# A feed-forward layer on attention outputs: the first product of one of eight batches as seven products of half blocks

## The chip, the cores and the metric

The kernel runs on one core of one Trainium2 chip. The metric is the device time of one execution in microseconds (us). The engines are named as in the profile: PE is TensorE's matmul stream and PEld its weight loads, DVE is VectorE, ACT is ScalarE, POOL is GpSimd, SP is SyncE, which here issues the DMAs.

## The reference

Attention with a local window and some global tokens is followed by a feed-forward layer with a softplus between its two products. Cut to what matters:

```python
# 8 batches, 8 heads, 512 local and 32 global tokens, head size 64
out_g = sm(scale * q_g @ k_all.T) @ v_all                 # global rows see all tokens
s_ll = where(abs(i - j) <= 32, scale * q_l @ k_l.T, -1e9) # local rows: window of 32 and the global keys
out_l = sm(concat([s_lg, s_ll])) @ concat([v_g, v_l])
x = concat([out_g, out_l]) as (4352 tokens, 512)
h = x @ w_in                                              # w_in 512 x 2048
g = maximum(h, 0.0) + log1p(exp(-abs(h)))
out = g @ w_out                                           # w_out 2048 x 512
```

## The kernel before

**Numbers.** Every float32 operand of the feed-forward layer is split into a high and a low part, and each product of two operands is done as three matmuls: high by high, high by the weight's low part, low by the weight's high part. The two weight matrices come as 64-bit numbers, are converted on the chip in the first fifth of the run and then stay in SBUF as 16 tiles `wi0` to `wi15` and 16 tiles `wo0` to `wo15` (128 partitions, high and low part of 512 columns each).

**Stages.** Batches 0 to 7 have 512 local tokens each; "batch 8" is the 256 global tokens of all batches. For a batch and each of 16 blocks f of 128 hidden columns, the first product `h` is 4 row blocks j of `w_in` by 3 parts, 12 matmuls with 512 moving columns (`hpart`), 192 in a batch; in batch 8 the moving side is 256 wide. `act` then makes the softplus and its two parts: ACT takes abs, exp and ln (L557 to L559), DVE adds relu(h) straight from PSUM (L560, `scalar_tensor_tensor`, which frees the bank of `h`), ACT rounds to `gh` (L563) and POOL subtracts to `gl` (L565). The second product (`second`, `opart`) adds up four PSUM tiles `o0` to `o3` over f; a half step of it is 6 matmuls of 512 columns. `store` copies the four tiles out on DVE and ACT (L585, L583) and sends them.

**Attention beside it.** The attention of head pair m (four in a batch, from m = 9 on in batches 1 to 6, ahead of the batch that uses it) is woven in as pieces: `both_scores` (PE `s_ps`, then on DVE the mask addition L329 and L327 and the block maxima L335), `maxima` and `probs` (POOL folds L360, DVE transposes, POOL subtracts L386, ACT exp, DVE sums L392), `totals` (POOL folds, DVE reciprocal, three copies L401 and the transpose `rb` L403) and `values` with `normalise` (PE `v_ps`, DVE L423 to L428). What makes the order is a list of slots: a batch has 48 units of time, head pair m has its pieces at `12*m` plus 5, 14 and 17.5, and `ORDER` weaves one batch's `H` (a block of `h`), `O` (a block of the second product) and `G` (scores of a pair). A scheduler then fixes each engine's row of instructions; `order` rows below show that row. An engine takes its row strictly in order.

**PSUM.** Two banks with the tag `h` hold the `h` tiles and also the second half of each `s_ps` (`s_ps*_1_0` and `s_ps*_1_1`); one pair of banks with the tag `a` holds the first half of `s_ps` (`s_ps*_0`) and `v_ps`; four banks hold `o0` to `o3`. So a block of `h` that follows a `G` waits until DVE has added the mask to `s_ps*_1_0` (the first L327), and `s_ps*_0` waits until `normalise` has read a preceding `v_ps`.

**Batch 7** has no attention left beside it: blocks of `h` alternate with blocks of the second product that lag one or two blocks behind.

## Time and profile before

| what | value |
| --- | --- |
| median of 3 runs | 974.57 us (974.49 to 975.27) |
| the profiled execution | 975.65 us, of which the span of the profile is 973.9 us |
| granted TensorE clock, mean | 0.991 of full speed |
| PE busy | 944.3 us, 97% of the span |
| PEld (weight loads) busy | 762.1 us, 78% |
| DVE busy | 620.9 us, 64% |
| ACT busy | 507.4 us, 52% |
| POOL busy | 448.9 us, 46% |
| batch 7, first `h` to the first `h` of batch 8 | 834.08 to 922.97 us of the span, 384 matmuls |

The profile lists what each engine was busy with, the chain of waits that ended last, groups of equal instructions (with the mean time of one, and the idle time before them), and on request a timeline. In a timeline row the first number is the start in us, the second the time until the last of `xN` instructions ended; matmuls overlap each other, so the pace of a run of them is read from start to start. A DVE row "idle before <- releaser" names what the engine waited for.

### The profile page before, as it was taken

To read this page: it belongs to the slowest core of one execution; us is meant where nothing else is said; L and a number is where in the kernel's file an instruction comes from. 1 tells how busy PE (TensorE), PEld (TensorE's weight loads), DVE (VectorE), ACT (ScalarE), POOL (GpSimd) and SP (SyncE) were. 2 spreads that over 40 slices of the span, in tenths; PEclk is the share of its full clock that TensorE was granted. 3 is DMA by queue.
4 is the path that set the end of the run, shared out by engine and by line. 5 is a ranking of instruction groups with operands and counts; after the bars stand their busy time and mean duration, and the time that the engine had idled before them with its cause. 6 is when DMAs were issued, how large, how long until landed. Compare 5 with 4: busy or idle time off the path is not lost.

```text
span 973.9 us, 14402 instructions
## 1 busy us (share of the span) xinstructions
PE 944.3 (97%) x5235; PEld 762.1 (78%) x5239; DVE 620.9 (64%) x1271; ACT 507.4 (52%) x914; POOL 448.9 (46%) x634
## 2 busy tenths in 40 slices
PE   6798899999999999999999999999999999999998
PEld 3676677778878888888888888888888888888896
DVE  6887948766667776677667667776677666211211
ACT  5787766644464444454454445444445446444453
POOL 5866967634444444344344444444435344122221
PEclk9899999999999999999999999999999999999999
DMA  9824321121102111121112101211112100100000
GB/s 355 327 77 164 108 77 51 60 79 47 50 18 93 50 50 50 50 94 50 46 38 93 50 21 47 93 50 50 50 50 91 35 18 18 50 1 1 20 25 23
DMA packets 34327, 66.21 MB, mean 68 GB/s; under 512 B 7632, under 2 KB 11472, under 8 KB 34256
## 3 DMA queue, kind: packets, MB, share of 16 engines
...
q14 instruction: 30, 0.25, 0.1%
...
## 4 chain that ended last, share of the span: by engine, by line
PE 86%; DVE 6%; ACT 4%; POOL 3%; issue 1%; DMA 0%; POOLq 0%; ACTq 0%; DVEq 0%
PE o L127 38%; PE h L127 36%; PE s_ps L127 6%; PE v_ps L127 5%; ACT e L174 1%; POOL s L386 1%; DVE sums L171 1%; DVE wbitswi L505 1%; DVE woraw L508 1%; DVE wbitswo L505 0%; PE s0g L127 0%; DVE wiraw L508 0%; POOL wi L515 0%; PE s L127 0%; DVE wbitswo L503 0%
## 5 line engine op out<-in xcount | busy, mean ns | idle before, releaser
L127 PE MATMUL h<-xh,wi 128*128 128x512 f32 (+1 forms) x1152 | 345.1, 383 | 3.5 <-DVE e L560 2.3
L127 PE MATMUL o<-wo,gh 128*128 128x512 f32 x1088 | 346.1, 399 | 0.4 <-POOL wo L515 0.4
L565 POOL TENSOR_TENSOR gl<-e,gh 128x512 fp32r<-128x512 f32 (+1 forms) x152 | 180.6, 1192 | 269.5 <-ACT gh L563 239.4
L127 PEld LDWEIGHTS h<-xh,wi 128*128 128x128 f32 x1152 | 213.1, 189 | 49.4 <-DVE e L560 3.2
L127 PEld LDWEIGHTS o<-wo,gh 128*128 128x128 f32 x1088 | 200.3, 188 | 48.7 <-POOL wo L515 0.8
L127 PE MATMUL o<-wo,gl 128*128 128x512 f32 x544 | 215.3, 396 | 4.3 <-POOL gl L565 4.3
L127 PE MATMUL h<-xl,wi 128*128 128x512 f32 (+1 forms) x576 | 219.4, 381 | 0.0
L560 DVE SCALAR_TENSOR_TENSOR e<-h,e 128x512 f32<-128x512 f32 x136 | 92.7, 681 | 185.1 <-ACT e L559 166.9
L557 ACT ACTIVATE e<-h 128x512 f32<-128x512 f32 x136 | 80.9, 595 | 214.5 <-PE h L127 214.4
L386 POOL TENSOR_TENSOR s<-s,mb 128x320 f32<-128x320 f32 (+6 forms) x136 | 138.9, 1057 | 72.7 <-DVE mb L382 72.7
L563 ACT CAST gh<-e 128x512 fp32r<-128x512 f32 x136 | 84.0, 617 | 117.6 <-DVE e L560 117.6
L127 PEld LDWEIGHTS h<-xl,wi 128*128 128x128 f32 x576 | 108.7, 189 | 22.5
L127 PEld LDWEIGHTS o<-wo,gl 128*128 128x128 f32 x544 | 102.4, 188 | 29.2 <-POOL gl L565 5.5
L559 ACT ACTIVATE e<-e,one 128x512 f32<-128x512 f32 x136 | 98.4, 724 | 3.9
L392 DVE TRANSPOSE_TENSOR_REDUCE zt<-s 128x32 f32<-128x1024 f32 x52 | 64.6, 1243 | 49.3 <-ACT s L388 49.3
L558 ACT ACTIVATE e<-e 128x512 f32<-128x512 f32 x136 | 85.9, 632 | 2.9
L388 ACT ACTIVATE s<-s 128x1024 f32<-128x1024 f32 x52 | 55.1, 1059 | 30.9 <-POOL mt L318 26.3
L335 DVE TRANSPOSE_TENSOR_REDUCE mt<-s 128x32 f32<-128x1024 f32 x52 | 64.7, 1244 | 5.5 <-ACT s L322 3.9
L127 PEld LDWEIGHTS s_ps<-raw 64*128 64x128 f32 x728 | 54.6, 187 | 11.4 <-issue 8.9
L360 POOL COPY mt<-mt 32x75 f32<-32x75 f32 x78 | 18.9, 242 | 92.3 <-DVE mt L335 90.1
L127 PE MATMUL s_ps<-raw 64*128 64x192 f32 (+3 forms) x728 | 60.2, 308 | 0.5
L382 DVE STREAM_TRANSPOSE mb<-mt 128x512 f32<-128x512 f32 (+1 forms) x104 | 52.6, 562 | 3.1 <-ACT mt L373 2.5
...
## 6 DMA issues: line engine op xcount, KB each, us to landing
...
```

Of the source, the lines that this page charges most:

```text
L127: order["pe"] = after(nc.tensor.matmul(*a, **k), "pe").ins
L335: order["scores"] = nc.vector.tensor_reduce(windows(st["mt", m], 4 + 16 * g, 36, 2, 16), s.rearrange("p h (b k) -> p h b k", k=32), axis=A ...
L382: nc.vector.transpose(mb[:, :, o:o + 32 * n].rearrange("p h (s k) -> p h s k", k=32), windows(e, k, 21, 2, n).unsqueeze(3).to_broadcast([P ...
L386: nc.gpsimd.tensor_tensor(s[:, h, o:o + w], s[:, h, o:o + w], mb[:, h, q:q + w], op=ALU.subtract)
L388: nc.scalar.activation(s, s, AF.Exp, scale=0.125)
L392: nc.vector.tensor_reduce(windows(st["zt", m], 4 + 16 * g, 36, 2, 16), s.rearrange("p h (b k) -> p h b k", k=32), axis=AX.X, op=ALU.add, a ...
L557: nc.scalar.activation(e, ph, AF.Abs)
L558: nc.scalar.activation(e, e, AF.Exp, scale=-1.0)
L559: nc.scalar.activation(e, e, AF.Ln, bias=one)
L560: nc.vector.scalar_tensor_tensor(e, ph, 0.0, e, op0=ALU.max, op1=ALU.add)
L563: nc.scalar.copy(gh, e)
L565: nc.gpsimd.tensor_tensor(gl[:, c], e[:, c], gh[:, c].bitcast(F32), op=ALU.subtract)
```

## The change

Batch 7's first product no longer runs as 192 matmuls of 512 columns. `x` (512 tokens by 512) and each fourth part of `w_in` are cut into halves both ways, and the eight products of half blocks are replaced by seven products of sums (the Winograd form of Strassen's method). A product of half blocks is 2 row blocks by 3 parts, 6 matmuls of 256 columns; for 8 pairs p of column blocks (p and p + 8) that makes 8 x 7 x 6 = 336 matmuls of 256 columns. `three`, `six` and `seventh` hold the products, each followed by copies and sums: ACT copies four quarter regions from PSUM to an SBUF tile `c` (in the slot `wi3`), DVE adds twice (the new L682 and L691), and `act` then reads `c` in place of PSUM.

The sums of `w_in` are made ahead. There are 16 steps `mix` at slots 118, 132, 146 and so on, which falls in batches 1 to 5: two POOL operations of 128x512, one DVE addition, one ACT rounding, one DVE subtraction, and one DMA of 512 KB to a DRAM scratch tensor. They share one tile (tag `cv`, one buffer), so a step that starts a new tile waits for the DMA of the step before. Sixteen `mix_out` DMAs write the unchanged blocks there as well. Batch 7 (28 blocks) and batch 8 (16 blocks) read their weights back by 44 DMAs of 512 KB through a ring of 12 tiles in the slots `wi4` to `wi15`; a block is loaded when the block 12 places before it has been used. The sums of `x` (`sums_x`, 14 POOL operations) and their rounding (`operand_x`, 11 ACT and 11 DVE operations) take the place of `split_x` for batch 7. The slots of the last two head pairs (30 and 31) move from +14 and +17.5 to +12 and +14.5, and the output tiles of batches 6 and 7 move to another tag.

The core of the diff:

```diff
...
+FAST = 7
+RING = 12
+MIX0, MIX1 = 118, 14
+ORDER7 = (1, 2, 5, 4, 6, 3, 7)
...
-            g0, g1, mx, tot, val = SLOTS.get(m, (None, None, 12 * m + 5, 12 * m + TOT, 12 * m + VAL))
+            t = (12 * m + 5, 12 * m + TOT, 12 * m + VAL) if m < M - 2 else (12 * m + 5, 12 * m + 12, 12 * m + 14.5)
+            g0, g1, mx, tot, val = SLOTS.get(m, (None, None) + t)
...
+        for i in range(16):
+            ps.append((MIX0 + MIX1 * i, lambda i=i: (mix_out(i), mix(*MIXES[i]))))
         ps.sort(key=lambda t: t[0])
         return ps
+    MIXES = [(q, u) for q in (2, 3, 0, 1) for u in ("S3", "S1", "S2", "S4")]
+    mixed = {}
+    def mix_out(k):
+        q, kk = k // 2 % 4, k // 8 * 2 + k % 2
+        tc.keep_in_program_order(nc.sync.dma_start(out=mix_dram[8 * q + (0, 1, 7, 3)[kk]], in_=wi[k].rearrange("p u c -> p (u c)").bitcast(F32)))
+    def mix(q, what):
+        a11, a12, a21, a22 = wi[2 * q], wi[2 * q + 1], wi[2 * q + 8], wi[2 * q + 9]
+        if what in ("S3", "S1"):
+            mixed["o"] = pl.tile([P, 2, 512], F32R, tag="cv", name=f"mix{q}{what}", bufs=1)
+        o = mixed["o"]
+        x, y, op = {"S3": (a11, a21, ALU.subtract), "S1": (a21, a22, ALU.add),
+                    "S2": (o, a11, ALU.subtract), "S4": (a12, o, ALU.subtract)}[what]
+        lo = o[:, 1].bitcast(F32)
+        tc.keep_in_program_order(nc.gpsimd.tensor_tensor(o[:, 0].bitcast(F32), x[:, 0].bitcast(F32), y[:, 0].bitcast(F32), op=op))
+        tc.keep_in_program_order(nc.gpsimd.tensor_tensor(lo, x[:, 1].bitcast(F32), y[:, 1].bitcast(F32), op=op))
+        nc.vector.tensor_tensor(lo, lo, o[:, 0].bitcast(F32), op=ALU.add)
+        nc.scalar.copy(o[:, 0], lo)
+        nc.vector.tensor_tensor(o[:, 1], lo, o[:, 0].bitcast(F32), op=ALU.subtract)
+        nc.sync.dma_start(out=mix_dram[8 * q + {"S1": 2, "S2": 4, "S4": 5, "S3": 6}[what]], in_=o.rearrange("p u c -> p (u c)").bitcast(F32))
+    plan = [8 * q + i for b in range(FAST, B) for q in range(4) for i in range(7)]
+    plan += [8 * (k // 2 % 4) + (0, 1, 7, 3)[k // 8 * 2 + k % 2] for k in range(NF)]
+    ring = {}
+    def load_ring(i):
+        if i < len(plan):
+            t = ring[i] = pl.tile([P, 2, 512], F32R, tag=f"wi{4 + i % RING}", name=f"ring{i}", bufs=1)
+            nc.sync.dma_start(out=t.rearrange("p u c -> p (u c)").bitcast(F32), in_=mix_dram[plan[i]])
...
+    sums, xs = {}, {}
+    def sums_x(b, k):
+        if k == 0:
+            t = pl.tile([P, 4, 2, 256], F32, tag="s", name=f"sums{b}", bufs=2)
+            sums[b] = {5: t[:, 0], 6: t[:, 1], 7: t[:, 2], 4: t[:, 3]}
+        t1, t2, t3, t4 = (sums[b][i] for i in (5, 6, 7, 4))
...
+        for f, o, n, w in SECOND:
+            a = windows(lower, 160 if o == 0 else 384, w, n, w)
+            nc.gpsimd.tensor_tensor(cut(t1, o, n, w), f(lower), a, op=ALU.subtract)
+            nc.gpsimd.tensor_tensor(cut(t2, o, n, w), f(upper), cut(t1, o, n, w), op=ALU.subtract)
+            nc.gpsimd.tensor_tensor(cut(t3, o, n, w), f(upper), f(lower), op=ALU.subtract)
+        nc.gpsimd.tensor_tensor(cut(t4, 0, 2, 128), half_1(upper), cut(t2, 0, 2, 128), op=ALU.subtract)
+    def operand_x(b, i):
+        s = ORDER7[i]
+        if i < 4:
+            x = [pl.tile([P, 2, 256], F32R, tag=f"x{u}{i}", name=f"x{u}{b}_{s}", bufs=1) for u in "hl"]
+        else:
+            t = pl.tile([P, 2, 2, 256], F32R, tag=f"wi{i - 4}", name=f"x{b}_{s}", bufs=1)
+            x = [t[:, 0], t[:, 1]]
+        xs[s] = x
+        if s in sums[b]:
+            t = sums[b][s]
+            nc.scalar.copy(x[0], t)
+            nc.vector.tensor_tensor(x[1], t, x[0].bitcast(F32), op=ALU.subtract)
+            return
...
-                        mm(ph[:, o:o + T], lhsT=wi[ff // 2 * 2 + j // 2][:, u, fs], rhs=xv[j][:, :T],
+                        k = ff // 2 * 2 + j // 2
+                        w = wi[k] if b < B else ring[len(plan) - NF + k]
+                        mm(ph[:, o:o + T], lhsT=w[:, u, fs], rhs=xv[j][:, :T],
                            start=(j == 0 and i == 0 and o == 0), stop=(j == 3 and i == 2), skip_group_check=True)
+            if b == B and js[0]:
+                release(len(plan) - NF + 2 * f)
+                release(len(plan) - NF + 2 * f + 1)
+        def release(k):
+            if k >= 0:
+                load_ring(k + RING)
+        def product(b, p, i, ps, start, stop):
+            k = 28 * (b - FAST) + 7 * (p // 2) + i
+            w, x = ring[k], xs[ORDER7[i]]
+            for j in range(2):
+                fs = slice(256 * j + p % 2 * P, 256 * j + p % 2 * P + P)
+                for n, (u, v) in enumerate(((0, 0), (1, 0), (0, 1))):
+                    mm(ps, lhsT=w[:, u, fs], rhs=x[v][:, j], start=start and j == 0 and n == 0, stop=stop and j == 1 and n == 2,
+                       skip_group_check=True)
+            if p % 2:
+                release(k)
+            if p == 7 and b < B - 1:
+                operand_x(b + 1, i)
+        def three(b, p):
+            t = [ps_h.tile([P, 512], F32, tag="h", name=f"h{b}_{p}_{u}") for u in range(2)]
+            X, N, Q, V = t[0][:, 0:256], t[0][:, 256:512], t[1][:, 0:256], t[1][:, 256:512]
+            if "c" not in g:
+                g["c"] = pl.tile([P, 2, 512], F32, tag="wi3", name="c", bufs=1)
+            c = g["c"]
+            product(b, p, 0, X, True, True)
+            nc.scalar.copy(c[:, 0, 0:256], X)
+            product(b, p, 1, Q, True, True)
+            product(b, p, 2, V, False, True)
+            nc.scalar.copy(c[:, 1, 256:512], V)
+            g["h"] = t, X, N, Q, V
+        def six(b, p):
+            (t, X, N, Q, V), c = g["h"], g["c"]
+            product(b, p, 3, N, False, True)
+            product(b, p, 4, X, False, True)
+            nc.scalar.copy(c[:, 1, 0:256], N)
+            nc.scalar.copy(c[:, 0, 256:512], X)
+            product(b, p, 5, V, False, True)
+            nc.vector.tensor_tensor(c[:, 0], t[1], c[:, 0], op=ALU.add)
+            g["ps", b, p] = c[:, 0]
+            g["X"] = X
+            act(b, p)
+        def seventh(b, p):
+            X, c = g["X"], g["c"]
+            product(b, p, 6, X, False, True)
+            d = c[:, 1].rearrange("p (n w) -> p n w", n=2)
+            nc.vector.tensor_tensor(d, X.unsqueeze(1).to_broadcast([P, 2, 256]), d, op=ALU.add)
+            g["ps", b, p + 8] = c[:, 1]
         def act(b, f):
             ph = g.pop(("ps", b, f))
...
-            if f == 0 and b > 0:
+            if f == 0 and b > 0 and not FAST <= b < B:
                 items.append((b, 0, 0, lambda b=b: [split_x(b, j) for j in range(4)]))
+            if FAST <= b < B:
+                if f < 8:
...
+                    items.append((b, 3, 0, lambda b=b, f=f: three(b, f)))
+                    if mid:
+                        second(done, b)
+                        done += 1
+                    items.append((b, 3, 0, lambda b=b, f=f: six(b, f)))
...
+                    for step in "OHOAOO":
+                        if step == "O":
+                            k0 = next(k, None)
+                            if k0 is not None:
+                                second(k0, b)
+                                done += 1
+                        elif step == "H":
+                            items.append((b, 1, 0, lambda b=b, f=f: seventh(b, f)))
+                        else:
+                            items.append((b, 0, 0, lambda b=b, f=f: act(b, f + 8)))
+                continue
...
+                            if b == FAST - 1 and f % 2 and f > 4:
+                                items.append((b, 0, 0, lambda f=f: (load_ring(f - 5), load_ring(f - 4))))
+                            if b == FAST - 1 and f == NF - 1:
+                                items.append((b, 0, 0, lambda b=b: [sums_x(b + 1, k) for k in range(2)]))
+                                items.append((b, 0, 0, lambda b=b: [operand_x(b + 1, i) for i in range(7)]))
                         elif what == "O":
                             second(done, b)
                             second(done + 1, b)
...
```

**End of batch 6, PE.** `o6_*` is the second product of batch 6 (here with `wo8`), `s_ps31` the scores of the last head pair, `v_ps30` the values of the pair before. Before:

```order
L127 MATMUL o6_3_7020<-wo8_1332,gh6_8_7403 128x512 x2
L127 MATMUL o6_3_7020<-wo8_1332,gl6_8_7404 128x512
L127 MATMUL s_ps31_0_7490<-raw31_0_7280 128x160 x2
L127 MATMUL s_ps31_0_7490<-raw31_0_7280 128x192 x2
L127 MATMUL s_ps31_0_7490<-raw31_1_7282 128x160 x2
L127 MATMUL s_ps31_1_0_7501<-raw31_1_7282 128x32
L127 MATMUL s_ps31_1_1_7502<-raw31_1_7282 128x32
```

Now:

```order
L133 MATMUL o6_3_7140<-wo8_1332,gh6_8_7531 128x512 x2
L133 MATMUL o6_3_7140<-wo8_1332,gl6_8_7532 128x512
L133 MATMUL v_ps30_7622<-s30_7390,v30_7258 64x160 x2
L133 MATMUL v_ps30_7622<-s30_7390,v30_7258 64x192 x8
L133 MATMUL v_ps30_7622<-s30_7390,v30_7258 64x96 x2
L133 MATMUL s_ps31_0_7643<-raw31_0_7404 128x160 x2
L133 MATMUL s_ps31_0_7643<-raw31_0_7404 128x192 x2
L133 MATMUL s_ps31_0_7643<-raw31_1_7406 128x160 x2
```

`v_ps30`, which stood behind the next block of `h`, now stands directly ahead of `s_ps31_0`, which uses the same banks.

**Start of batch 3, DVE.** `zt16` and `rb16` are the totals of pair 16, `s17` the masked scores of pair 17, `e3_f` the softplus of batch 3, block f. Before:

```order
L560 SCALAR_TENSOR_TENSOR e3_1_4046<-h3_1_4033,e3_1_4046 128x512
L367 COPY zt16_3911<-zt16_3911 32x6
L397 TENSOR_SCALAR zt16_3911<-zt16_3911 32x42
L398 RECIPROCAL zt16_3911<-zt16_3911 32x42
L401 COPY zt16_3911<-zt16_3911 32x21 x3
L403 STREAM_TRANSPOSE rb16_4098<-zt16_3911 128x640
L560 SCALAR_TENSOR_TENSOR e3_2_4068<-h3_2_4055,e3_2_4068 128x512
L329 TENSOR_TENSOR s17_4117<-s_ps17_0_4108,mask_72 128x2x512
L335 TENSOR_REDUCE mt17_4115<-s17_4117 128x2x16
L327 TENSOR_TENSOR s17_4117<-s_ps17_1_0_4119,mask_72 128x512
L327 TENSOR_TENSOR s17_4117<-s_ps17_1_1_4120,mask_72 128x512
```

Now, with `mix3S1` a tile of the sums of `w_in`:

```order
L700 SCALAR_TENSOR_TENSOR e3_2_4121<-h3_2_4108,e3_2_4121 128x512
L373 COPY zt16_3957<-zt16_3957 32x6
L485 TENSOR_TENSOR mix3S1_3776<-mix3S1_3776 128x512
L403 TENSOR_SCALAR zt16_3957<-zt16_3957 32x42
L404 RECIPROCAL zt16_3957<-zt16_3957 32x42
L335 TENSOR_TENSOR s17_4170<-s_ps17_0_4161,mask_72 128x2x512
L407 COPY zt16_3957<-zt16_3957 32x21 x3
L341 TENSOR_REDUCE mt17_4168<-s17_4170 128x2x16
L409 STREAM_TRANSPOSE rb16_4151<-zt16_3957 128x640
L333 TENSOR_TENSOR s17_4170<-s_ps17_1_0_4172,mask_72 128x512
L333 TENSOR_TENSOR s17_4170<-s_ps17_1_1_4173,mask_72 128x512
L341 TENSOR_REDUCE mt17_4168<-s17_4170 128x2x16
```

The three copies of `zt16` and the transpose to `rb16` stood ahead of the mask additions of `s17`; the copies and the transpose are now between them and the one that frees the `h` bank (`s_ps17_1_0`), and the mix's subtraction stands ahead of all.

**The same place, POOL.** `gl3_f` is the low part of batch 3's block f. Before:

```order
L565 TENSOR_TENSOR gl3_0_4006<-e3_0_4000,gh3_0_4005 128x512
L360 COPY zt16_3911<-zt16_3911 32x75 x3
L565 TENSOR_TENSOR gl3_1_4052<-e3_1_4046,gh3_1_4051 128x512
L391 MEMSET zt18_4408 128x3x4
L565 TENSOR_TENSOR gl3_2_4074<-e3_2_4068,gh3_2_4073 128x512
L360 COPY mt17_4115<-mt17_4115 32x75 x3
```

Now:

```order
L705 TENSOR_TENSOR gl3_0_4052<-e3_0_4046,gh3_0_4051 128x512
L481 TENSOR_TENSOR mix3S1_3776<-mix3S1_3776,wi6_822 128x512
L482 TENSOR_TENSOR mix3S1_3776<-mix3S1_3776,wi6_822 128x512
L366 COPY zt16_3957<-zt16_3957 32x75 x3
L705 TENSOR_TENSOR gl3_1_4105<-e3_1_4099,gh3_1_4104 128x512
L705 TENSOR_TENSOR gl3_2_4127<-e3_2_4121,gh3_2_4126 128x512
```

The two POOL operations of the mix stand ahead of the copies of `zt16`, by which DVE starts its totals.

**Start of batch 7, PE.** Before, `h7_0` is the whole first block:

```order
L127 MATMUL o6_1_6997<-wo15_1937,gh6_15_7721 128x512 x2
L127 MATMUL o6_1_6997<-wo15_1937,gl6_15_7722 128x512
L127 MATMUL h7_0_7818<-xh7_0_7782,wi0_289 128x512 x2
L127 MATMUL h7_0_7818<-xl7_0_7783,wi0_289 128x512
L127 MATMUL h7_0_7818<-xh7_1_7788,wi0_289 128x512 x2
L127 MATMUL h7_0_7818<-xl7_1_7789,wi0_289 128x512
```

Now, from the fifth product of the first pair on (`h7_0_0` and `h7_0_1` are two banks with the quarter regions, `ring0` to `ring6` its weights):

```order
L133 MATMUL h7_0_0_7976<-x7_6_7925,ring4_7557 128x256 x6
L133 MATMUL h7_0_1_7977<-x7_3_7928,ring5_7559 128x256 x6
L133 MATMUL o6_0_7113<-wo15_1937,gh6_15_7861 128x512 x2
L133 MATMUL o6_0_7113<-wo15_1937,gl6_15_7862 128x512
L133 MATMUL o6_1_7117<-wo15_1937,gh6_15_7861 128x512 x2
L133 MATMUL o6_1_7117<-wo15_1937,gl6_15_7862 128x512
L133 MATMUL h7_0_0_7976<-x7_7_7937,ring6_7730 128x256 x6
L133 MATMUL o6_2_7136<-wo15_1937,gh6_15_7861 128x512 x2
L133 MATMUL o6_2_7136<-wo15_1937,gl6_15_7862 128x512
L133 MATMUL o6_3_7140<-wo15_1937,gh6_15_7861 128x512 x2
L133 MATMUL o6_3_7140<-wo15_1937,gl6_15_7862 128x512
L133 MATMUL h7_1_0_8066<-xh7_1_7905,ring0_7316 128x256 x2
```

Three products of a pair stand ahead of the second product's half steps and then three more; at the first pair all six run in one piece, and behind them there are only the two half steps of batch 6's last block.

More of the change, by code (lines that the diff above doesn't have):

```diff
@@ new lines, in moe_over_global_local_attention @@
+    SECOND = ((lambda t: t[:, 0:128].unsqueeze(1), 0, 1, 128), (lambda t: windows(t, 288, 224, 2, 64), 128, 2, 64))
+    sums, xs = {}, {}
[4 more added lines that the diff above has]
+        t1, t2, t3, t4 = (sums[b][i] for i in (5, 6, 7, 4))
+        assert (b, k) in ready and (b, k + 2) in ready
+        lower, upper = xa[b, k], xa[b, k + 2]
+        cut = lambda t, o, n, w: t[:, k, o:o + n * w].rearrange("p (n w) -> p n w", n=n)
+        for f, o, n, w in SECOND:
[4 more added lines that the diff above has]
+        nc.gpsimd.tensor_tensor(cut(t4, 0, 2, 128), half_1(upper), cut(t2, 0, 2, 128), op=ALU.subtract)
@@ new lines, in operand_x @@
+    def operand_x(b, i):
[11 more added lines that the diff above has]
+            return
+        for k in range(2):
+            t = xa[b, k + (0 if s == 1 else 2)]
+            for f, o, n, w in SECOND if s == 3 else ((half_1, 0, 2, 128),):
+                hi, lo = (y[:, k, o:o + n * w].rearrange("p (n w) -> p n w", n=n) for y in x)
+                nc.scalar.copy(hi, f(t))
+                nc.vector.tensor_tensor(lo, f(t), hi.bitcast(F32), op=ALU.subtract)
@@ L529, in moe_items @@
     def moe_items():
-        tiles = [(b, f) for b in range(B) for f in range(NF)] + [(B, f) for f in range(NF // 2)]
+        order7 = [f + 8 * u for f in range(NF // 2) for u in range(2)]
+        tiles = [(b, f) for b in range(B) for f in (order7 if b >= FAST else range(NF))] + [(B, f) for f in range(NF // 2)]
         g, po, items = {}, {}, []
@@ L585, in store @@
                 nc.vector.tensor_copy(o, po[t])
-            if b < B:
+            if FAST <= b < B:
+                x0 = 0
+                for r, n in ROWS7[t]:
+                    r += b * S + SG
+                    nc.sync.dma_start(out=out[r:r + n, :], in_=o[x0:x0 + n])
+                    x0 += n
+            elif b < B:
                 r = b * S + SG + t * P
@@ L602, in moe_items @@
         for i, (b, f) in enumerate(tiles):
-            if f == 0 and b > 0:
+            if f == 0 and b > 0 and not FAST <= b < B:
                 items.append((b, 0, 0, lambda b=b: [split_x(b, j) for j in range(4)]))
+            if FAST <= b < B:
+                if f < 8:
+                    late = 2 * tiles.index((b, f)) - done
+                    assert late == 4 or (b, f) == (FAST, 0) and late <= 4, (b, f, late)
+                    mid = late == 4
+                    items.append((b, 3, 0, lambda b=b, f=f: three(b, f)))
[3 more added lines that the diff above has]
+                    items.append((b, 3, 0, lambda b=b, f=f: six(b, f)))
+                    k = iter(range(done, done + late - mid))
+                    for step in "OHOAOO":
[6 more added lines that the diff above has]
+                            items.append((b, 1, 0, lambda b=b, f=f: seventh(b, f)))
+                        else:
+                            items.append((b, 0, 0, lambda b=b, f=f: act(b, f + 8)))
+                continue
             if 0 < b < B - 1:
```

11 lines of the change are left out of this document (10 added, 1 removed).

## The prediction

> **What bounds the kernel now.** I read the page first: the busy times, the slices, the chain that ended last.
>
> ```profile
> PE 944.3 (97%) x5235; PEld 762.1 (78%) x5239; DVE 620.9 (64%) x1271; ACT 507.4 (52%) x914; POOL 448.9 (46%) x634
> ...
> PE   6798899999999999999999999999999999999998
> ...
> DVE  6887948766667776677667667776677666211211
> ...
> GB/s 355 327 77 164 108 77 51 60 79 47 50 18 93 50 50 50 50 94 50 46 38 93 50 21 47 93 50 50 50 50 91 35 18 18 50 1 1 20 25 23
> ...
> PE 86%; DVE 6%; ACT 4%; POOL 3%; issue 1%; DMA 0%; POOLq 0%; ACTq 0%; DVEq 0%
> ```
>
> From the sixth slice of PE to the last but one there is nothing but nines: TensorE never waits, and a matmul taken away there is time taken away. DVE is at six to seven tenths in batches 1 to 6 and at one to two tenths in batch 7 (the last six slices), so batch 7 has room beside PE and the earlier batches have less. The view by stretches shows the same for batch 7 and for a piece of batch 3.
>
> ```profile
> 834.08:922.97 88.89, 88.89 (x386) 72.14 (x385) 15.20 (x23) 44.46 (x70) 20.64 (x16) 1.00 0.04 14
> ...
> 450.00:500.00 50.00, 50.00 (x272) 40.44 (x269) 35.71 (x78) 22.40 (x35) 23.13 (x34) 1.00 0.16 49
> ```
>
> After the length the columns are PE, PEld, DVE, ACT and POOL, then the granted clock. In batch 7 DVE works 15.20 of 88.89 us; in the earlier piece it works 35.71 of 50 us, always at full clock. So this change takes from a place where only PE is short and gives DVE and POOL work where they are nearer to their limit.
>
> **Part 1: the matmuls of batch 7.** In the timeline of PE I read the pace from start to start: the first `h` of batch 7, the first of batch 8 (256 wide), and what follows two blocks of 24 in batch 8.
>
> ```profile
> 834.08 0.63 PE L127 MATMUL h<-xh,wi 128*128 128x512 f32 x2
> ...
> 922.97 0.40 PE L127 MATMUL h<-xh,wi 128*128 128x256 f32 x2
> ...
> 925.75 0.62 PE L127 MATMUL o<-wo,gh 128*128 128x512 f32 x2
> ...
> 929.97 0.40 PE L127 MATMUL h<-xh,wi 128*128 128x256 f32 x2
> ...
> 932.80 0.64 PE L127 MATMUL o<-wo,gh 128*128 128x512 f32 x2
> ```
>
> 384 matmuls of 512 columns in 922.97 - 834.08 = 88.89 us are 0.2315 us each. 24 of 256 columns took 2.78 us (922.97 to 925.75) and 2.83 us (929.97 to 932.80), 0.117 us each on the mean. So 192 x 0.2315 = 44.4 us go and 336 x 0.117 = 39.3 us come: **-5.1 us**. By 0.116 and 0.118, the two blocks' own means, it is -5.4 to -4.8.
>
> **Part 2: the seams of batch 7.** A block's way from its last matmul to both parts of `g` is seen on one block of batch 7:
>
> ```profile
> 903.01 1.28 POOL L565 TENSOR_TENSOR gl<-e,gh 128x512 fp32r<-128x512 f32 x1 [4.18 <-ACT gh L563]
> ...
> 904.81 0.63 PE L127 MATMUL o<-wo,gh 128*128 128x512 f32 x2
> 905.06 0.60 ACT L557 ACTIVATE e<-h 128x512 f32<-128x512 f32 x1 [2.13 <-PE h L127]
> ...
> 905.70 0.63 ACT L558 ACTIVATE e<-e 128x512 f32<-128x512 f32 x1
> ...
> 906.36 0.72 ACT L559 ACTIVATE e<-e,one 128x512 f32<-128x512 f32 x1
> ...
> 907.19 0.69 DVE L560 SCALAR_TENSOR_TENSOR e<-h,e 128x512 f32<-128x512 f32 x1 [4.91 <-ACT e L559]
> ...
> 907.91 0.62 ACT L563 CAST gh<-e 128x512 fp32r<-128x512 f32 x1 [0.83 <-DVE e L560]
> ```
>
> From the last matmul to ACT's start it is 0.25 us, then 0.60, 0.63, 0.72, 0.69, 0.62 and 1.28 us. The new way has one DVE addition ahead of it, for which I take the 0.69 of L560, the same shape. For p = 1 to 6 the six products of a pair end, then come 2.1 us (half step and seventh), two half steps (2.8) and the next three products (2.1): 7.0 us and the first two matmuls (0.47) until the low part is wanted. It needs 0.25 + 0.69 + 0.60 + 0.63 + 0.72, then ACT's abs and exp of the other block, which stand ahead of `gh` (1.23; L560's 0.69 runs beside them), 0.62 and 1.28, together 6.0 and some 6.3 with its handovers: no stall, 1.2 us to spare. ACT's work per pair, 2 x (0.60 + 0.63 + 0.72 + 0.62) and four copies of 256 columns, at most the 0.62 of the twice as wide L563 each, is 7.6 of the 10.5 us that a pair takes on PE (42 x 0.117 + 24 x 0.2315), DVE's four operations 2.8, POOL's two 2.6: none is a bound there.
>
> At the two ends it does not fit. At p = 7 the next pair's three products are missing, so that the low part is wanted at 4.9 + 0.5 = 5.4 and is there at 6.3: **+0.9**. At p = 0 the four output tiles of batch 6 are copied in between, priced by the same copies before:
>
> ```profile
> 833.58 0.69 DVE L585 COPY ot<-o 128x512 f32<-128x512 f32 x1 [1.43 <-PE o L127]
> ...
> 834.28 0.59 ACT L583 COPY ot<-o 128x512 f32<-128x512 f32 x1 [2.72 <-PE o L127]
> ```
>
> Counted from the start of batch 7, the six end at 4.2, the low part is wanted at 4.2 + 1.4 + 0.7 + 1.4 + 2.1 + 0.5 = 10.3. DVE's addition ends at 5.1, abs at 5.8; ACT's copy 6.4, exp 7.1, ln 7.8; DVE's second copy holds L560 until 7.9, it ends at 8.6; ACT takes abs, copy and exp first (9.6), then `gh` 10.3 and POOL `gl` 11.6. **+1.4**. If the scheduler's row is harmless at both ends, both are nothing.
>
> **Part 3: end of batch 6.** `v_ps30` stands right ahead of `s_ps31_0`, which needs its banks. What has to be read out first is seen on pair 31:
>
> ```profile
> 828.21 1.64 PE L127 MATMUL v_ps<-s,v 128*64 128x192 f32 x20
> ...
> 829.89 0.42 DVE L423 TENSOR_TENSOR xa<-v_ps,rb 128x256 f32<-128x256 f32 x1 [3.55 <-PE v_ps L127]
> 830.24 0.21 DVE L424 TENSOR_TENSOR lap<-v_ps,rb 128x64 f32<-128x64 f32 x1
> ...
> 830.37 0.51 DVE L425 TENSOR_TENSOR xa<-v_ps,rb 128x352 f32<-128x352 f32 x1
> ```
>
> `v_ps` ends at 829.85, the last read at 830.88; with the handover PE stands **1.15 us**. Behind it DVE is that much late for the additions that free the `h` banks of the two last blocks; I take **0.4** of it (0 to 1.15). Nothing covers this: PE's row is strict.
>
> **Part 4: the sums of `w_in`.** Per step: POOL 2 x 1.28 = 2.6 us, DVE 2 x 0.69 = 1.4, ACT 0.62; 16 steps in five batches, where DVE has some 30% free. The cost is not the sum but what stands ahead of an operation for which PE waits. One place, the start of batch 3, before:
>
> ```profile
> 417.16 0.79 POOL L360 COPY zt<-zt 32x75 f32<-32x75 f32 x3
> ...
> 419.75 0.40 DVE L398 RECIPROCAL zt<-zt 32x42 f32<-32x42 f32 x1
> ...
> 420.19 0.54 DVE L401 COPY zt<-zt 32x21 f32<-32x21 f32 x3
> ...
> 420.76 0.84 DVE L403 STREAM_TRANSPOSE rb<-zt 128x640 f32<-128x640 f32 x1
> ...
> 420.90 0.72 ACT L559 ACTIVATE e<-e,one 128x512 f32<-128x512 f32 x1
> ...
> 421.65 0.69 DVE L560 SCALAR_TENSOR_TENSOR e<-h,e 128x512 f32<-128x512 f32 x1
> ...
> 422.96 1.23 DVE L329 TENSOR_TENSOR s<-s_ps,mask 128x1024 f32<-128x1024 f32 x1 [0.62 <-PE s_ps L127]
> ...
> 424.22 1.25 DVE L335 TRANSPOSE_TENSOR_REDUCE mt<-s 128x32 f32<-128x1024 f32 x1
> ...
> 425.39 1.25 DVE L327 TENSOR_TENSOR s<-s_ps,mask 128x512 f32<-128x512 f32 x2
> ...
> 426.81 0.63 PE L127 MATMUL h<-xh,wi 128*128 128x512 f32 x2
> ```
>
> The bank that `h3_3` needs is free when the first of the two L327 is done, 425.39 + 0.63 = 426.02; PE comes at 426.81. So the cover is 0.79 us. Now the POOL pair shifts the `zt` copies to 419.7 and their end to 420.5, so the totals can't be done ahead of L560 at 421.65. After it (422.3) come a small copy and the mix's subtraction (423.2), the scalar step and reciprocal (423.8), L329 (425.0), the three copies (425.6), L335 (426.8), `rb` (427.7), L327 (428.3): `h3_3` starts at 428.4, **+1.6**. At the end of batch 4 ACT's row has the mix's rounding (0.62) and one exp (0.63) ahead of `gh` of block 14, and the scores of pair 24 wait for the block behind it: **+1.25**. Of the other 14 steps eight stand behind what PE waits for and cost nothing; in six a DVE pair stands ahead of it, 1.38 - 0.79 = 0.59 at most beyond the cover, at least nothing; I take 0.4, nearer to the cover measured, **+2.4** (0 to 3.5; if that cover were gone 6 x 1.38 = 8.3).
>
> The 32 writes and 44 reads of 512 KB run beside this: batch 7 needs 7 blocks in two pairs, 3.7 MB in 21 us, 175 GB/s, where the first slices show 327 and 355 and batch 7's own 1 to 50. I cost them at nothing. On SP a mix's DMA waits for its subtraction with the loads of later pairs queued behind it; these come a pair ahead, so 1 to 2 us hide.
>
> **The sum:** -5.1 + 0.9 + 1.4 + 1.15 + 0.4 + 1.6 + 1.25 + 2.4 = **+4.0 us**. On the profiled execution, 975.65 us (973.9 of span and 1.75 around it), that is 979.65; its time is 1.08 above the median, so I forecast **978.6** for a median of 974.57. What the measurement can tell from no change is 0.2%, 1.95 us.
>
> **The rivals.** *The cover holds everywhere outside batch 7* (0.28): parts 3 and 4 cost nothing, because DVE finds more than 1.4 us idle ahead of the additions that free a bank; in favour are the 14 us of idle DVE in the 50 us shown, against it the 0.79 read above. Then -5.1 + 0.9 + 1.4 = -2.8, 971.8 us, faster; without the seams 969.5.
>
> *Half of it is covered* (0.17): part 3 and the batch 3 place stay, the rest hides: -2.8 + 1.55 + 1.6 = +0.35, 974.9, no difference.
>
> *The weight loads set the pace of narrow matmuls* (0.02). Twice as narrow, a matmul still loads 128 columns of weights:
>
> ```profile
> L127 PEld LDWEIGHTS h<-xh,wi 128*128 128x128 f32 x1152 | 213.1, 189 | 49.4 <-DVE e L560 3.2 <-ACT xa L232 1.4 <-issue 0.3
> ```
>
> At 0.189 us each, 336 x 0.189 = 63.5 us would come for 44.4, +19, and with the other terms 1003 us. The blocks of batch 8 ran at 0.117 with one load for each, so they overlap. [...]
>
> **The numbers.** The forecast and its neighbours (some stalls from 2 us of loss upward) have 0.53, so slower 0.55, same 0.17, faster 0.28. The low end is the first rival with one seam gone, 970.5; the high end takes the six steps without cover, 978.6 + 5.9 = 984.5. Beyond them lie the rest of the first rival and the weight loads, under 0.2.
>
> **What would show it.** In the changed profile: a pace of 0.117 in batch 7's `h` and its length near 86 us; PE idle ahead of `h` blocks in batches 1 to 5 by 5 us in all, released by DVE; about 1.2 us ahead of `s_ps` at the end of batch 6; two waits for `gl` at the ends of batch 7. If PE shows no idle time in batches 1 to 6, part 4 is wrong; if batch 7 is no shorter, part 1 is.

## The result and the profile after

The changed kernel takes 991.27 us (median of 5 runs, 991.09 to 994.18) beside 974.8 us of the kernel before (5 runs): 1.0176 of it, 95% interval 1.0165 to 1.0188. It is slower, as forecast, but by 16.5 us where 4.0 were forecast, and outside the range.

The page of the changed kernel, the lines that answer to those shown of before:

```profile
PE 946.2 (96%) x5379; PEld 767.5 (78%) x5383; DVE 674.7 (68%) x1323; ACT 526.1 (53%) x966; POOL 502.7 (51%) x680
...
PE   6898899999999999999999999989999999999998
...
DVE  6888957767678677777777777788767667533311
...
PE 50%; DVE 18%; issue 12%; POOL 12%; ACT 8%; DMA 1%; POOLq 0%; ACTq 0%; DVEq 0%
```

PE was 86% of the chain that ended last and is 50% now; DVE and POOL stand for 30%. The nines hide it, since a wait of 1 us is little in a slice of 25. The view of PE's waits from 200 us on (engine, line, what it waited for; us in total, times, longest) shows it, where the kernel before has no row at all:

```profile
PE s_ps L133 <- DVE e L700: 8.1, 6, 2.7
PE h L133 <- DVE s L333: 3.4, 4, 1.0
PE h L133 <- DVE e L700: 1.3, 1, 1.3
PE o L133 <- POOL gl L705: 1.2, 2, 0.6
PE s_ps L133 <- issue: 1.1, 1, 1.1
PE h L133 <- DVE xl L553: 0.8, 1, 0.8
```

PE waits for DVE: for the relu (`e`, L700) that frees a bank which the scores need, for the mask addition (L333) that frees the bank of the next `h`, and once for an operand (`xl`). Most waits cost 0.3 to 0.4 us more than their row (the first one's row says 0.97, and the pair loses 1.3): in an unbroken run a matmul of 512 columns starts every 0.23 us and takes 0.39, so that they overlap; at the first wait one starts at 265.24, the next at 266.60 and the next at 266.93, 1.69 us for two starts in place of 0.46.

Where the time goes is read from the starts of the scores (`s_ps`) of each pair in both traces. Up to pair 11 the changed kernel is 0.8 us ahead (a difference of the start-up), then it loses by pairs, in us: 12 +1.3, 13 +1.5, 14 +1.5, 18 +1.2, 19 +0.9, 20 +0.9, 22 +1.0, 25 +2.7, 26 +4.6, 27 +1.2, all others up to pair 30 0.1 or less. That is **16.9 us in batches 1 to 5**, where the steps on `w_in` stand. To these come the end of batch 6 and batch 7, in the timeline of PE:

```profile
814.92 1.28 PE L133 MATMUL s_ps<-raw 64*128 64x160 f32 x16 [1.14 <-issue]
...
838.10 0.74 PE L133 MATMUL h<-xh,wi 128*128 128x512 f32 x2 [1.32 <-DVE e L700]
...
862.60 0.50 PE L133 MATMUL o<-wo,gl 128*128 128x512 f32 x1 [0.62 <-POOL gl L705]
...
934.94 0.50 PE L133 MATMUL o<-wo,gl 128*128 128x512 f32 x1 [0.62 <-POOL gl L705]
```

1.14 + 1.32 = 2.5 us are lost at pairs 30 and 31. From the first matmul of batch 7 to the last of all it is 984.43 - 851.44 = 132.99 us, against 968.82 - 834.08 = 134.74 before, though the changed kernel has one half step (1.4 us) of batch 6 more in it: **3.2 us gained**. 16.9 + 2.5 - 3.2 - 0.8 = 15.4, the 15.5 us by which the span grew.

The worst place is the end of pair 25 (listed at pair 26), on POOL, DVE and PE:

```profile
644.50 1.29 POOL L705 TENSOR_TENSOR gl<-e,gh 128x512 fp32r<-128x512 f32 x1 [3.52 <-ACT gh L703]
644.59 3.68 DVE L407 COPY zt<-zt 32x21 f32<-32x21 f32 x3
...
645.76 1.26 POOL L481 TENSOR_TENSOR mix1S<-wi,wi 128x512 f32<-128x512 f32 x1
...
646.99 1.25 POOL L482 TENSOR_TENSOR mix1S<-wi,wi 128x512 f32<-128x512 f32 x1
...
649.08 0.65 DVE L700 SCALAR_TENSOR_TENSOR e<-h,e 128x512 f32<-128x512 f32 x1
...
649.78 1.33 PE L133 MATMUL s_ps<-raw 64*128 64x32 f32 x14 [2.69 <-DVE e L700]
```

Three copies of 32x21 took 3.68 us, one for each of POOL's three operations; behind them stands the relu for which PE waits 2.69 us. The prediction has one price for such copies, the 0.54 of the row at 420.19, at another place. The kernel before has long copies as well, where they cost nothing:

```profile
387.76 1.29 POOL L565 TENSOR_TENSOR gl<-e,gh 128x512 fp32r<-128x512 f32 x1 [1.50 <-issue]
...
388.32 1.14 DVE L401 COPY zt<-zt 32x21 f32<-32x21 f32 x3
```

Of the 4.6 us at pair 26 the wait is 2.7. Behind it the granted clock is 0.50 for 3.41 us (the first 0.50 in the view of this stretch, the first row below), and matmuls of 512 columns start every 0.43 us in place of 0.23:

```profile
651.09:654.50 3.41, 3.41 (x9) 2.74 (x9) 3.41 (x4) 0.62 (x1) 0.64 (x1) 0.50 0.50 149
...
652.06 0.63 PE L133 MATMUL o<-wo,gl 128*128 128x512 f32 x1
652.49 1.05 PE L133 MATMUL o<-wo,gh 128*128 128x512 f32 x2
```

That is 1.6 us more. It does not change the sum: e2 (below) has the same wait of 2.69 us without such a stretch, loses 3.3 us at pair 26 and 2.6 at pair 27, where the changed kernel loses 1.2.

Not every wait goes straight back to DVE. Ahead of three of the eleven (at 293.98, 482.52 and 621.81) the relu had itself waited for ACT, in whose row the step's rounding (L484) stands:

```profile
479.14 0.62 ACT L484 CAST mix0S<-mix0S 128x512 fp32r<-128x512 f32 x1 [0.71 <-DVE mix0S L483]
...
481.77 0.69 DVE L700 SCALAR_TENSOR_TENSOR e<-h,e 128x512 f32<-128x512 f32 x1 [0.96 <-ACT e L699]
```

### The profile page after: what moved, and what is told of

It is laid out like the page before. It is cut to its first block, busy times and chain, and to the rows that moved or that the text cites. A ratio compares the mean times of both kernels' runs of the same rounds, so it can differ in the third digit from the quotient of the medians.

```text
span 989.4 us, 15052 instructions
## 1 busy us (share of the span) xinstructions
PE 946.2 (96%) x5379; PEld 767.5 (78%) x5383; DVE 674.7 (68%) x1323; ACT 526.1 (53%) x966; POOL 502.7 (51%) x680
## 4 chain that ended last, share of the span: by engine, by line
PE 50%; DVE 18%; issue 12%; POOL 12%; ACT 8%; DMA 1%; POOLq 0%; ACTq 0%; DVEq 0%
PE o L133 21%; PE h L133 21%; POOL s L392 4%; POOL gl L705 4%; PE s_ps L133 3%; PE v_ps L133 3%; DVE mt L341 3%; DVE e L700 1%; DVE s L335 1%; DVE zt L407 1%; DVE s L333 1%; ACT e L697 1%; ACT e L698 1%; ACT e L699 1%; ACT e L180 1%
## 5 line engine op out<-in xcount | busy, mean ns | idle before, releaser
L705 POOL TENSOR_TENSOR gl<-e,gh 128x512 fp32r<-128x512 f32 (+1 forms) x152 | 183.7, 1213 | 239.8 <-ACT gh L703 219.9
L133 PE MATMUL h<-xh,wi 128*128 128x512 f32 x896 | 283.5, 398 | 6.8 <-DVE s L333 3.4
L133 PEld LDWEIGHTS h<-xh,wi 128*128 128x128 f32 x896 | 168.5, 189 | 48.7 <-DVE s L333 5.4
L133 PE MATMUL h<-xl,wi 128*128 128x512 f32 x448 | 176.8, 395 | 0.8 <-DVE xl L553 0.8
L392 POOL TENSOR_TENSOR s<-s,mb 128x320 f32<-128x320 f32 (+6 forms) x136 | 139.3, 1059 | 71.9 <-DVE mb L388 71.9
L697 ACT ACTIVATE e<-h 128x512 f32<-128x512 f32 x120 | 71.3, 594 | 176.6 <-PE h L133 175.3
L700 DVE SCALAR_TENSOR_TENSOR e<-h,e 128x512 f32<-128x512 f32 x120 | 81.7, 681 | 101.3 <-ACT e L699 87.6
L133 PEld LDWEIGHTS h<-xl,wi 128*128 128x128 f32 x448 | 84.8, 189 | 21.0 <-DVE xl L553 1.3
```

The source lines that it names most:

```text
L133: order["pe"] = after(nc.tensor.matmul(*a, **k), "pe").ins
L392: nc.gpsimd.tensor_tensor(s[:, h, o:o + w], s[:, h, o:o + w], mb[:, h, q:q + w], op=ALU.subtract)
L697: nc.scalar.activation(e, ph, AF.Abs)
L700: nc.vector.scalar_tensor_tensor(e, ph, 0.0, e, op0=ALU.max, op1=ALU.add)
L705: nc.gpsimd.tensor_tensor(gl[:, c], e[:, c], gh[:, c].bitcast(F32), op=ALU.subtract)
```

## The experiments

The theories. **1**, the steps' arithmetic makes PE wait; **1a**, because DVE's operations between SBUF tiles are held up while POOL works, as the copies above (3.68 us at 644.59, 0.54 at 420.19); **1b**, because the added operations simply stand in DVE's row. **2**, the traffic of 76 transfers of 512 KB does. **3**, it depends on where in a pair's pattern a step stands; **4**, DVE and POOL are too full anyway. Each run stands beside the kernel before, measured together with it:

| run | us | kernel before | ratio, 95% interval |
| --- | --- | --- | --- |
| e1 no sums | 976.46 | 975.51 | 1.0014 (1.0004 to 1.0023) |
| e2 sums only | 993.19 | 975.51 | 1.0186 (1.0167 to 1.0205) |
| e3 POOL's part | 980.94 | 975.51 | 1.0073 (1.0047 to 1.0098) |
| e4 DVE's part | 992.37 | 975.51 | 1.0175 (1.0156 to 1.0194) |
| e5 distance 12, phase 7 | 985.09 | 974.62 | 1.0101 (1.0087 to 1.0115) |
| e6 and pair 30 back | 982.16 | 974.62 | 1.0078 (1.0064 to 1.0093) |
| e7 distance 12, phase 0 | 1012.09 | 974.62 | 1.0383 (1.0368 to 1.0398) |
| e8 DVE's part in place | 978.04 | 974.62 | 1.0035 (1.0022 to 1.0048) |
| e9 phase 7, reductions | 975.58 | 974.96 | 1.0008 (0.9999 to 1.0016) |
| e10 all in free places | 976.25 | 974.96 | 1.0011 (1.0002 to 1.0020) |
| e11 and seams | 974.64 | 974.96 | 0.9999 (0.9990 to 1.0008) |
| e12 own slots, reductions | 984.60 | 974.96 | 1.0099 (1.0085 to 1.0113) |
| e13 before with reductions | 974.86 | 974.87 | 1.0002 (0.9993 to 1.0011) |
| e14 POOL's part, reductions | 979.66 | 974.87 | 1.0045 (1.0028 to 1.0063) |
| e15 all pieces together | 970.97 | 974.87 | 0.9963 (0.9950 to 0.9977) |

**Arithmetic or traffic?** In e1 the body of `mix` is only the DMA of an unsummed block: it leaves the sums out, so its products are not those of the layer. In e2 the steps are added to the kernel before. The diff is e1's (`...` stands for the end of a line):

```diff
+        src = {"S3": a21, "S1": a22, "S2": a11, "S4": a12}[what]
+        nc.sync.dma_start(out=mix_dram[...], in_=src...)
```

> The changed kernel with the arithmetic of the sixteen steps on w_in left out: no POOL, DVE or ACT operation of a step, the unsummed block is written to DRAM instead, so that all 32 writes, all 44 reads, the 336 narrow matmuls and the moved pieces of pairs 30 and 31 stay. It computes the products with the wrong weights, and is there for its time alone. Theory 1 (queue and shared access: the steps' operations on POOL and DVE delay what TensorE waits for) expects the 16.9 us that the trace shows lost between the scores of pair 11 and pair 31 to be gone: 991.3 - 16.9 = 974.4 us. Theory 2 (DMA traffic: the writes and reads of 512 KB slow the loads and stores of the kernel) expects most of the loss to stay, 985 us or more.

> The kernel before, with the sixteen steps on w_in and the 32 writes added at the same slots and nothing else changed; their results are not used. Theory 1 expects the whole loss of batches 1 to 5, 16.9 us: 974.8 + 16.9 = 991.7 us. The prediction's own pricing of the steps, 5.3 us, would give 980.1 us. Theory 2, with the writes but without the 44 reads, expects a part of the loss, 980 to 986 us.

e1 lost 1.0 us, e2 17.7. In e1's trace the pairs 12 to 27 lose nothing, so the 2.1 us beyond the expected 974.4 lie elsewhere; e2 loses 17.1 us in them, at the same pairs as the changed kernel (12 +1.4, 13 +1.5, 14 +1.5 and so on to 27). The 32 writes and 44 reads cost nothing that shows; theory 2 is out, and so is the prediction's price.

**Which engine's part?** All three are the kernel before with parts of the steps added. e3 leaves out `mix`'s DVE and ACT lines, e4 and e8 its POOL lines. The diff shows what e4 and e8 change in `mix` (the lines are shown without `bitcast` and `keep_in_program_order`; e8 keeps the new line in the order of the program, e4 does not):

```diff
-        nc.gpsimd.tensor_tensor(o[:, 0], x[:, 0], y[:, 0], op=op)
-        nc.gpsimd.tensor_tensor(lo, x[:, 1], y[:, 1], op=op)
-        nc.vector.tensor_tensor(lo, lo, o[:, 0], op=ALU.add)
+        nc.vector.tensor_tensor(lo, x[:, 0], y[:, 0], op=op)
```

> As the kernel before with the sixteen steps, but only their two POOL operations and the writes, without the two DVE operations and the ACT rounding of a step (the sums are left unrounded and unused). Theory 1a (shared access: DVE's copies between SBUF tiles do not run while POOL works, as three copies of 32x21 that took 3.68 us beside POOL at 644.59 against 0.54 us elsewhere) expects at least half of the loss here: 983 to 988 us. Theory 1b (plain queueing: DVE's added operations stand ahead of the mask additions and of relu) expects little here, 975 to 978 us.

> As the kernel before with the sixteen steps, but without the two POOL operations of a step: DVE makes the first one from the blocks themselves, then ACT's rounding, DVE's subtraction and the writes stay (half of the sum is left out). Theory 1a expects little here, 975 to 979 us, since POOL has no new work; theory 1b expects most of the loss, 984 us or more.

> As the run of the kernel before with DVE's and ACT's part of the steps alone, but held to the order of the program: in that run the scheduler had put several steps among the weight conversions at the end of batch 0 (11 us of its loss lie there). Theory 1b (DVE's own operations in the queue make the loss) expects 8 to 14 us over the kernel before, in batches 1 to 5. Theory 1a (DVE is held up by POOL's added work) expects under 4 us.

e4 does not answer: with nothing to hold them, the scheduler put its operations among the weight conversions, and in its trace 14.5 us are lost ahead of pair 9 (there, too, the granted clock is 0.50 for 13.65 us from 200.21 on). e8 holds them and loses 3.4 us, e3 5.4 us (its executions lie between 979.73 and 985.22): together 8.8, half of 17.7. So neither engine's added work makes the loss by itself. Either the two act on each other, or e8's steps, which need not wait for POOL, stand at cheaper places; these runs alone don't decide it. In e3 DVE has no operation more, and yet its own are slow beside POOL's:

```profile
287.59 4.36 DVE L495 TENSOR_TENSOR xl<-xa,xh 128x128 fp32r<-128x128 f32 x5 [1.37 <-ACT xh L494]
...
288.21 1.35 POOL L476 TENSOR_TENSOR mix2S<-wi,mix2S 128x512 f32<-128x512 f32 x1
...
289.52 1.61 POOL L477 TENSOR_TENSOR mix2S<-wi,mix2S 128x512 f32<-128x512 f32 x1
```

Five subtractions of two SBUF tiles (three of 128x128 and two of 128x384) took 4.36 us. In the kernel before the same five take 0.29 and 0.56 each and 2.3 us from the first to the last (286.06 to 288.37), with POOL at rest. POOL's second operation took 1.61 in place of 1.29.

**Place.** e5, e7 and e6 change numbers only:

```diff
-MIX0, MIX1 = 118, 14
+MIX0, MIX1 = 115, 12        # e5, e6; e7: 120, 12
-            t = (...) if m < M - 2 else (12 * m + 5, 12 * m + 12, 12 * m + 14.5)
+            t = (...) if m < M - 1 else (12 * m + 5, 12 * m + 12, 12 * m + 14.5)   # e6
```

> The changed kernel with the sixteen steps at slots 115, 127, 139 and so on (first 115, distance 12) in place of 118 and 14; nothing else is changed. A pair's scores, maxima, totals and values come every 12 units, so with a distance of 14 the steps drift through the pairs' pattern; with 12 each stands at the same place, and DVE's two operations of a step come behind the sums L398 and ahead of the transpose to rb and of one more relu, where the trace of the changed kernel shows four steps (behind the scores of pairs 14, 15, 21 and 22) that cost TensorE nothing. Theory 3 (place: the loss is set by where in a pair's pattern the operations stand, not by how many there are) expects all of the 16.9 us to go: 991.3 - 16.9 = 974.4 us, within 1 us of the kernel without the sums. Theory 4 (load: with 16 steps DVE and POOL are too full in batches 1 to 5, whatever the place) expects 985 us or more.

> As the run with the steps 12 units apart, but the first at slot 120, so that all sixteen stand just ahead of or inside a pair's mask additions. Theory 3 expects every step to cost what the costly ones of the changed kernel do, 0.9 to 1.5 us each: 974.4 + 16 x 1.2 = 994 us, more than the changed kernel. Theory 4 expects the same time as at the other phase.

> As the run with the steps 12 units apart, and the slots of pair 30 back at +14 and +17.5, so that its values product stands behind the next block of the first product again and not directly ahead of the scores of pair 31; pair 31 keeps its earlier slots. If the wait of 1.14 us ahead of these scores and that of 1.32 us ahead of the last block of batch 6 come from this, both go: 2.5 us less than the run before, about 972 us, faster than the kernel before by the 3.2 us of batch 7. If the earlier place of pair 31's values is what makes the second wait, only 1.1 us go.

With sixteen equal steps the kernel lies 10.5 us above the one before at one phase and 37.5 at another: theory 4 is out. In e7's trace the pairs from 12 on lose 40.4 us, of which up to 12 are clock: it is 0.50 in five stretches, 23.9 us together, each at or within 2 us behind a wait of PE of 1.4 to 2.7 us. Waits as long have none in other traces (2.7 us in e2, 1.9 in e5), so what brings such a stretch on stays open. But theory 3 had promised nothing left at phase 7, and e5 has four waits, at pairs 14, 18, 22 and 26, 2.2 us each (the other twelve steps cost nothing), one at 319.69:

```profile
313.06 2.51 POOL L705 TENSOR_TENSOR gl<-e,gh 128x512 fp32r<-128x512 f32 x2 [3.17 <-PE o L133]
...
313.26 2.53 DVE L407 COPY zt<-zt 32x21 f32<-32x21 f32 x3
...
318.98 1.25 DVE L333 TENSOR_TENSOR s<-s_ps,mask 128x512 f32<-128x512 f32 x2
...
319.69 0.74 PE L133 MATMUL h<-xh,wi 128*128 128x512 f32 x2 [1.93 <-DVE s L333]
```

The step has made DVE 2.3 us late; because of that its copies now meet POOL's `gl`, and lose 2.0 us more. Before they had come at a time when POOL rested. e6 is 2.9 us below e5; both waits at pairs 30 and 31 are gone.

**Exclusion.** The three copies become reductions, which the changed kernel's trace shows unslowed (32x12 from 32x96, 0.30 to 0.33 us with a POOL operation beside them and 0.30 to 0.33 without; for the pairs from 9 on, `WIDE` being 9):

```diff
-            small(m)(e[32 * a:32 * a + 32, 0:21], e[0:32, o:o + 21])
+            nc.vector.tensor_reduce(e[32 * a:32 * a + 32, 0:21], e[0:32, o:o + 21].unsqueeze(2), axis=AX.X, op=ALU.max)  # m >= WIDE
```

> As the run with the steps at slots 115, 127 and so on, with one change: the three small copies of the totals (32x21, ahead of the transpose to rb) are done as reductions over an axis of length one, which the trace shows unslowed beside POOL (a 32x12 reduction takes 0.30 us each with and without it), where the copies took 2.53 us in place of 0.54 beside two POOL operations. DVE's row is the same, operation for operation. That run has four waits of 2.2 us left in batches 2 to 5. Theory 1a (DVE's copies are shut out while POOL works) expects about 2.0 us of each to go, 985.1 - 8 = 977 us; theory 1b (only the time of the added operations in the row) expects no change, 985 us.

> The changed kernel at its own slots with the three small copies as reductions. Theory 1a expects the copies' excess where it stands ahead of a mask addition or a relu (1.1 us at 316.89, 1.1 at 534.70, 3.1 at 644.59, a part of which the wait behind it hides) to go: 4 to 5 us less, 986 to 987 us. Theory 1b expects 991 us. More than 6 us would mean that other copies count as well.

> The kernel before with the three small copies of the totals as reductions over an axis of length one, and nothing else: the control for the other runs with reductions. In the kernel before these copies take 1.13 to 1.29 us beside POOL at most places and 0.54 elsewhere, but TensorE never waits from 200 us on, so both theories expect no change, 974.8 us within 1 us.

> The kernel before with POOL's two operations of the sixteen steps and the writes alone (980.9 us, 5.4 over its kernel before in that call), with the three copies as reductions. Theory 1a (what POOL's operations cost is that they shut DVE's copies out) expects most of the 5.4 us to go: 975 to 977 us. If POOL's operations cost by standing ahead of the low parts and the folds in POOL's own row, 980 us stay.

e9 has e5's row on DVE, operation for operation, and is 9.5 us faster. Between the two traces 8.0 of them stand at these four pairs, as expected; no run shows where the rest lies. The same place:

```profile
315.81 2.51 POOL L708 TENSOR_TENSOR gl<-e,gh 128x512 fp32r<-128x512 f32 x2 [3.17 <-PE o L133]
...
316.02 0.53 DVE L410 TENSOR_REDUCE zt<-zt 32x21 f32<-32x21 f32 x3
...
319.74 1.25 DVE L333 TENSOR_TENSOR s<-s_ps,mask 128x512 f32<-128x512 f32 x2
...
320.44 0.74 PE L133 MATMUL h<-xh,wi 128*128 128x512 f32 x2
```

Beside the same two `gl` the reductions take 0.53 us, and PE's wait has shrunk from 2.2 us to 0.2. This is theory 1a, shown for the copies: 2.53 us as copies, 0.53 as reductions. The control e13 is unchanged, so the reductions gain nothing where PE does not wait. In the changed kernel itself they bring 6.7 us (e12 against 991.27). In the traces 4.9 of them lie in the pairs 12 to 27 (a loss of 12.1 in place of 16.9), which is the 4 to 5 expected, and 1.7 ahead of pair 9, where no copy was changed. With POOL's part alone (e14) the loss is 4.8 us where e3 has 5.4, and the executions of the two runs overlap; most had been expected to go. Two of e14's three waits (at 294.30 and 617.91) stand behind `xl` subtractions held up as above, which the reductions don't touch, and the longer of them is followed by 3.41 us at a clock of 0.50. At the third (431.29) no operation of DVE is slowed: there POOL's two operations stand ahead of the folds in POOL's own row.

**Free places and all together.** e10 and e11 build on e6; e15 has the steps of e5, unmoved:

```diff
-            ps.append((MIX0 + MIX1 * i, ...))
+            ps.append((MIX0 + MIX1 * i - (3 if i % 4 == 3 else 0), ...))    # e10, e11
-                    for what in ORDER:
+                    for what in ORDER if b < FAST - 1 else ORDER[:-1]:      # e11, e15
-            if f == 0 and b > 0:
+            if f == 0 and 0 < b < B:                                        # e11, e15
```

> As the run with the steps 12 units apart and pair 30's slots back, but every fourth step 3 units earlier (148, 196, 244, 292), which is the place behind a batch's last mask additions where one step of the changed kernel cost nothing (POOL 3.3 us, DVE 6.1 us behind the scores of pair 20). The copies stay copies. Theory 3 (place alone) expects the four waits of 2.2 us to go: 982.2 - 8.8 = 973.4 us, between 972 and 975. If DVE or POOL is simply too full, a like amount comes back elsewhere: 980 us or more.

> As the run with all steps in free places, and the two ends of batch 7 eased: batch 6 leaves one more block of the second product for batch 7's first pair, and batch 8's first block comes ahead of the last pair's first half step. The two waits for the low part (0.6 us each in the trace of the changed kernel, some 1.0 us each with the restart of PE) should go: 2 us less than the run before, 971.4 us. If x's operands are not ready 2.8 us earlier, a wait at the start of batch 7 takes that back.

> The pieces put together: the steps at slots 115, 127 and so on, the three copies as reductions, pair 30's slots back, and both ends of batch 7 eased. From the run with phase 7 and reductions (975.6 us): less the 2.5 us at pairs 30 and 31, less the 1.7 us that the seams gave, 971.4 us, 3.4 us faster than the kernel before. If the four waits of 0.2 us grow, or a new one comes at batch 7's start, 973 us.

e10 is 5.9 us below e6, not 8.8: at pairs 14, 18, 22 and 26 1.0 us each is left, again by copies beside POOL, now ahead of the relu:

```profile
313.39 1.28 POOL L705 TENSOR_TENSOR gl<-e,gh 128x512 fp32r<-128x512 f32 x1 [2.29 <-ACT gh L703]
313.44 1.63 DVE L407 COPY zt<-zt 32x21 f32<-32x21 f32 x3
315.11 0.69 DVE L700 SCALAR_TENSOR_TENSOR e<-h,e 128x512 f32<-128x512 f32 x1
...
315.85 1.33 PE L133 MATMUL s_ps<-raw 64*128 64x32 f32 x14 [0.56 <-DVE e L700]
```

e11 gains 1.6 us at both ends of batch 7. e15 takes phase 7, the reductions, pair 30's slots and the ends together: 970.97 us where 971.4 were expected, 0.9963 of the kernel before (0.9950 to 0.9977). Its page has PE's nines back, with fewer us busy than the kernel before:

```profile
PE 942.2 (97%) x5383; PEld 765.5 (79%) x5383; DVE 659.1 (68%) x1323; ACT 525.2 (54%) x966; POOL 504.2 (52%) x680
...
PE   6898899999999999999999999999999999999997
```

## Why the prediction was wrong

**Part 1 was right.** The first 36 narrow matmuls of batch 7 take

```profile
851.44:855.69 4.25, 4.25 (x37) 4.24 (x36) 0.00 (x0) 1.26 (x4) 0.00 (x0) 1.00 0.00 0
```

4.25 us, 0.118 each (0.117 forecast). So the rival by the weight loads, 0.189 us each, is out.

**Part 2 was right in kind.** Both waits for `gl` are there, 0.62 us each and some 0.9 with what a wait costs beside its row; 2.3 us were forecast (the working's own figures, 10.3 and 11.6, make 1.3 and not 1.4 at the first end), and 1.6 went with them in e11. Batch 7 as a whole gained 3.2 (2.8 forecast).

**Part 3 was too small.** The wait ahead of the scores is 1.14 (1.15 forecast; its row names no releaser), but the delay of DVE behind it reached the next block in full, 1.32 in place of 0.4; e6 shows that both hang on pair 30's slots.

**Part 4 failed.** It forecast 5.25 us; it was 16.9. Eleven waits of PE with 12.3 us in their rows are there, where 5 us ahead of `h` blocks were forecast; six of them stand ahead of scores. The two places worked out were right in kind. At the start of batch 3 (pair 18, +1.2, 1.6 forecast) no operation is slowed, and the row alone makes the loss, as worked out. At the end of batch 4 the relu waits for ACT behind the step's rounding, as worked out, but PE's row there says 1.65. The step's two POOL operations hold up five `xl` subtractions, which took 2.3 us in the kernel before, and another `xl`, held up by POOL's L392, costs 0.82 at 634.36 (pair 25, +2.7 together, 1.25 forecast).

```profile
614.27 3.84 DVE L553 TENSOR_TENSOR xl<-xa,xh 128x128 fp32r<-128x128 f32 x5 [2.04 <-ACT xh L552]
...
621.81 1.33 PE L133 MATMUL s_ps<-raw 64*128 64x32 f32 x14 [1.65 <-DVE e L700]
```

The other fourteen steps cost 13.0 where 2.4 were taken. The step that failed is their price, the fixed durations of a step's own operations less a cover of 0.79 us: "in six a DVE pair stands ahead of it, 1.38 - 0.79 = 0.59 at most beyond the cover". DVE's durations were not fixed here. POOL's work lengthened what DVE did meanwhile, the step's own pair as well, at this place beside the `gl` that stands behind the step on POOL:

```profile
680.75 1.76 DVE L483 TENSOR_TENSOR mix1S<-mix1S 128x512 f32<-128x512 f32 x1
```

It takes 0.65 to 0.69 at 13 of its 16 places, and a late DVE meets POOL at other places than before. That was to be seen in the trace of before: the three copies take 0.54 us at five of 23 places, of which 420.19 is one, and 1.13 to 1.29 beside POOL's `gl` at the others, as at 388.32. The prediction read the one row and did not ask what a copy costs beside POOL.

The runs tell the copies from the reductions: the three copies take 0.54 to 3.68 us in the changed kernel and 2.53 beside two `gl` in e5, the reductions 0.53 beside the same two in e9. Why POOL holds up the one and not the other was not shown.

How the 16.9 us divide is settled in part only. The copies are 4.9 (e12). In the trace of the changed kernel an operation held up by POOL stands in DVE's row right ahead of seven of the eleven waits: the copies at 319.27, 537.10 and 649.78, the step's own pair at 266.60, 458.95 and 683.17, `xl` at 634.36. What holds it up is POOL's `gl` at five of them, which the kernel before has as well, L392 at 634.36, and `gl` with the step's own two operations at 649.78. Ahead of three stands ACT's rounding, at 621.81 with slowed `xl` before it, and ahead of one, 431.45, the row alone. For all but the copies this is read from durations; no run takes the slowing away and leaves the work.

Of the rivals, the one where the cover holds everywhere is what e15 comes to by design; it then gave 3.9 us, where that rival has 5.1 without the waits at the ends of batch 7. In its trace 0.9 us are left at pairs 14, 18, 22 and 26.
